# Seven-product channel mixing: the second products of a pair of batches one pass later, a third of them between first products, and raw weights and spills on GpSimd's queue

## The chip, the cores and the metric

The kernel runs on one core of one Trainium2 chip. The core has TensorE (PE; its weight loads are listed apart as PEld), VectorE (DVE), ScalarE (ACT), GpSimd (POOL) and SyncE (SP, here a queue of DMA issues alone). Each takes its instructions in order. The metric is device time in microseconds of one execution, as the median of several; lower is better.

## The reference

Three layers follow one another on float32 data with 4 batches, 448 positions and 768 channels:

```
scores = q @ k^T / 8 - log(448);  x = sigmoid(scores) @ v       # 12 heads of 64
h  = x^T @ U @ V;  u = x + h^T                                  # over positions, rank 32
x2 = u + max(u @ w_ch1, 0) @ w_ch2                              # 768 -> 3072 -> 768
theta = x2 @ w_theta
y  = w_tok_r @ (x2 * cos(theta)) + w_tok_i @ (x2 * sin(theta))
u2 = x2 + y;  out = u2 + max(u2 @ w_ch, 0)
```

The weights arrive as float64. The change concerns the line with w_ch1 and w_ch2, and the conversion of the weights of the layers behind it, which goes on beside it.

## The kernel before

**Precision.** TensorE multiplies fp32r operands. Each float32 operand is split into a high and a low part, and each product is three matmuls: high x high, high x low, low x high (`half_product`, L860 to L868; `Y`, L884 to L902).

**Steps and pairs.** The hidden 3072 channels are handled in 12 steps (i = 0 to 11) of 256. A step needs 256 columns of w_ch1 (two jobs, w1_i_0 and w1_i_1) and 256 rows of w_ch2 (two jobs, w2_i_0 and w2_i_1). The 4 batches are two pairs (pr = 0, 1). One step for one pair is called a pass here; it is the function `phase` (L964). A pass has first products (u @ w_ch1, then relu into tiles h) and second products (h @ w_ch2, added to the resident X): for each of the two batches three pieces `Y(..., e2)` of 12 matmuls, "thirds" here. A third goes into one of two banks y, and VectorE adds it to X (L897).

**Seven products.** Steps 0 and 1 take four plain quadrants a pass. From step 2 on, a pass takes the 2 x 2 block product with seven half products of 9 matmuls (b11, b21, t2, t1, b22, t3, t4) in place of eight. Their left operands b11, t1 and so on are made from w1 by VectorE and ScalarE, with low halves by GpSimd. Their right operands are X's splits, or sums s1 to s4 of X's quarters. The sums are made in steps 0 and 1 and written to DRAM (`s_d`); in each pass `load_s` (L913) reads each of the four sets back, three DMAs of 448 KB a set, into a ring of six tiles, so two sets are in memory at a time. A set's load goes out when the set that held its tiles has been used: s3 after t2 (which uses s1), s2 after t1 (s0), the next pass's s1 after b22, its s0 after t3. The program's names count from zero (s_1_3 is set 3 of pair 1).

**Copies.** Partial sums are kept in PSUM banks a, b and d and are reused. ScalarE copies p1, u2 and p5 out (L997) before the next product goes on accumulating in the same bank; VectorE adds the copy to another bank (`both`, L1001), and `relu` (L870) makes h.

**Conversion jobs.** Every weight is a `Conv` job (L126) with steps. `load` brings the raw words into one of two ws tiles, `size` (ScalarE, L151) makes an estimate of the value, `bits`, `top`, `word` (VectorE, L155 to L165) put the exact float32 together in one of three ca tiles, and a finish makes high and low parts. A job's `load_ahead` issues the raw load of the job two places on; it takes place after `word`, or for theta after the finish, since that job's finish uses the ws tile as scratch. Such a load waits until VectorE has done the step. Extra jobs convert the later layers' weights and spill them to DRAM: 6 for theta, 7 for w_tok, 12 halves of w_ch in 6 jobs. The tables `place` and `place_extra` (L650 to L697) set at which place (i, b, t) of the program a step of a job is recorded, and `tick` records them there.

**Queues.** Behind the attention layer, raw loads, spills, s loads and the writes of s all go out from SP, in program order.

Of the kernel before, what the change touches and what calls it, by code (L numbers as in the profile page):

```python
# [24 lines left out]
def tile_kernel(  # L25
# [101 lines left out]
    class Conv:  # L127
        def __init__(self, key, pp, n, dma, fin, turns=False, more=(), dest=None):
            self.key, self.pp, self.n, self.dma = key, pp, n, dma
            self.turns, self.dest, self.fin = turns, dest, fin  # L130
            self.next = None
            self.steps = [self.size, self.bits, self.top, self.word, *([self.finish] if fin else []), *more]
            self.ahead = self.finish if turns else self.word

        def step(self):
            now = self.steps.pop(0)
            now()
            if now == self.ahead:
                self.load_ahead()
# [66 lines left out]
    def loader():  # L206
        return nc.sync if "sp" in late else nc.gpsimd
# [94 lines left out]
    def conv_wc(kk, s):  # L302
# [55 lines left out]
    def conv_tok(i):  # L358
# [22 lines left out]
        def spill():  # L381
            nc.sync.dma_start(out=tok_d[:, :, i, :], in_=st["o"])
# [264 lines left out]
    extra = th_jobs + [(f"tok{i}", conv_tok(i)) for i in range(NZ)]  # L647
    extra += [(f"wc{kk}_{s}", conv_wc(kk, s)) for kk in range(NH3) for s in range(2)]
# [13 lines left out]
    def place_extra(i, b):  # L662

        name, job = extra.pop(0)
        queue(name, job)
        for t in range(1, 4):
            at(i, b, t, name)
        ts = (0, 2, 4) if job.turns else (0, 2) if len(job.steps) == 6 else (0, 1, 3, 4)
        if not job.turns:
            at(i, b, 4, name)  # L670
        for t in ts:
            at(i, b + 1, t, name)

    place(0, 2, ("w1", 1, 0), conv_w1(1, 0))
    place(0, 3, ("w1", 1, 1), conv_w1(1, 1))
    name = ("w2", 1, 0)
    queue(name, conv_w2(1, 0))
    for t in range(1, 5):
        at(0, 3, t, name)
    at(1, 0, 0, name)  # L680
    for i in range(1, NB):
        more = 1 < i < L
        place(i, 0, ("w2", i, 1), conv_w2(i, 1), (0, 3))
        if more:
            place_extra(i, 0)
        if i == L:
            break
        place(i, 1, ("w2", i + 1, 0), conv_w2(i + 1, 0))
        if more:
            place_extra(i, 1)  # L690
        place(i, 2, ("w1", i + 1, 0), conv_w1(i + 1, 0))
        if i == L - 1:
            place_extra(i, 2)
        name = ("w1", i + 1, 1)
        place(i, 3, name, conv_w1(i + 1, 1))
        if i + 1 >= PLAIN:
            for t in range(2, 5):  # L697
                at(i, 3, t, name)
# [241 lines left out]
    def s_split(n, part):  # L940
        pr, kk = divmod(n, K3)
        (s2, s4), (s3, s1) = ((a[:, 0], a[:, 1]) for a in s_job[n])
        for x, s in (((2, s2), (1, s1)), ((4, s4), (3, s3)))[part]:
# [6 lines left out]
    def do(i, b, t):  # L950
        n = 4 * i + b - 2
        if 0 <= n < 2 * K3:
            if t == 0:
                s_load(n)
            elif t == 2:
                s_sums(n)
            elif t > 2:
                s_split(n, t - 3)
        tick(i, b, t)

    def ticks(i, b):
        return lambda e2: do(i, b, e2 + 2)

    def phase(i, pr, prev):  # L964
        b = 2 * pr

        def last(e2):
            if prev is not None:
                Y(*prev, 1, e2, ticks(i, b))

        def mine(e2):
            Y(i, pr, 0, e2, ticks(i, b + 1))

        if i < PLAIN:
            quadrant(i, pr, 0, 0, lambda: do(i, b, 0))
            quadrant(i, pr, 0, 1, lambda: do(i, b, 1))
            for e2 in range(NK // 2):
                if prev is None:
                    do(i, b, e2 + 2)
                last(e2)  # L980
            quadrant(i, pr, 1, 1, lambda: do(i, b + 1, 0))
            quadrant(i, pr, 1, 0, lambda: do(i, b + 1, 1))
            if i == PLAIN - 1:
                for x in (1, 0)[pr:pr + 1]:
                    load_s(0, x)
            for e2 in range(NK // 2):
                mine(e2)
            return
        w = {x: w1_t[i, x] for x in ("b11", "b21", "b22", "t1", "t2", "t3", "t4")}
# [10 lines left out]
        def both(o, t):  # L1000
            nc.vector.tensor_add(t, o, t)  # L1001
            return t
        a, bb, d = (bank_g(f"{x}_{i}_{pr}") for x in "abd")
# [8 lines left out]
        if (i, pr) == (L, 1):  # L1012
# [5 lines left out]
        if (i, pr) == (L, 1):  # L1018
            load_th(2, False)
        last(1)  # L1020
        half_product(d, w["b22"], xs_q[pr, 3], False)
# [3 lines left out]
        last(2)  # L1025
        half_product(a, w["t3"], xs_q[pr, 2], False)
        if more:
            load_s(nxt[1], 0)
        if (i, pr) == (L, 1):
            load_th(3, False)  # L1030
        relu((i, pr, 1, 1), both(a, p5), lambda: do(i, b + 1, 0))
        mine(0)
        half_product(a, w["t4"], a22, False)
        relu((i, pr, 1, 0), a, lambda: do(i, b + 1, 1))
# [591 lines left out]
```

## Time and profile before

| | us |
|---|---|
| median of 3 runs | 1230.09 |
| lowest, highest | 1225.1, 1232.09 |
| profiled execution | 1226.73 |
| its span | 1223.9 |
| PE busy / PEld busy | 1125.2 / 969.0 |
| DVE busy | 805.1 |
| ACT busy | 444.3 |
| POOL busy | 323.2 |
| TensorE's mean granted clock (1 is full) | 0.970 |

The profile is of one execution. Busy time is the time in which an instruction of the engine ran; matmuls overlap, so PE's busy time says little of how many matmuls ran, and the count beside it says more. PEclk is the granted clock of TensorE in a stretch, as a share of full speed. DMA is the mean busy share of the core's 16 DMA engines. A wait is listed with the engine and line that waited, and with what released it.

### The profile page before, as it was taken

Reading aid. Unit: us, or ns where it says so; the run is one execution under the profiler, and the core shown is the slowest. Engines: PE = TensorE matmul, PEld = TensorE weight load, DVE = VectorE, ACT = ScalarE, POOL = GpSimd, SP = SyncE. Lnnn points to the kernel's source line nnn. Section 1 sums busy time; section 2 is a strip of 40 time slices with the busy share of each in tenths; the row PEclk is TensorE's granted clock in tenths of the full one; section 3 lists DMA queues with packets and bytes.
Section 4 is the critical chain, followed back from the end, with each engine's and each line's share of the span. In section 5 each row is a group of like instructions: output and inputs, shape, how many; then the busy total and the mean of one; then the engine's idle time right before and its main releaser. Section 6 shows DMA issues by size and latency. Waiting matters only on the chain. (4 is left out here: it accounts for less than half of the span.)

```text
span 1223.9 us, 16968 instructions
## 1 busy us (share of the span) xinstructions
PE 1125.2 (92%) x6183; PEld 969.0 (79%) x6183; DVE 805.1 (66%) x1138; ACT 444.3 (36%) x697; POOL 323.2 (26%) x340
## 2 busy tenths in 40 slices
PE   8999989898898989999999989797899999999997
PEld 5554478897777777888888878686798999999997
DVE  5878785877656566656566766567566645564785
ACT  6887752333232222322222233233220534341330
POOL 6412052112121112121212222223312323230273
PEclk9999999899898999999899989899799999999999
DMA  9999527678676778878777786776777732081333
GB/s 169 158 198 189 89 95 248 236 276 342 208 272 204 266 267 273 286 239 285 239 268 256 271 297 246 257 288 226 285 263 276 224 52 40 1 261 36 79 70 71
DMA packets 267794, 254.23 MB, mean 208 GB/s; under 512 B 170928, under 2 KB 222576, under 8 KB 267584
## 3 DMA queue, kind: packets, MB, share of 16 engines
q1 hardware_dynamic: 255600, 231.82, 60.7%
q0 software_dynamic: 8256, 20.87, 6.2%
q10 hardware_dynamic: 3856, 0.48, 0.3%
q8 instruction: 48, 0.79, 0.3%
q14 instruction: 34, 0.28, 0.1%
HBM read 206.83 MB, written 44.89 MB: 206 GB/s over the span
## 5 line engine op out<-in xcount | busy, mean ns | idle before, releaser
L893 PE MATMUL y<-h,w 128*128 128x448 f32 x576 | 215.5, 374 | 15.5 <-DVE X L897 14.9
L894 PE MATMUL y<-h,w 128*128 128x448 f32 x576 | 213.3, 370 | 0.0
L895 PE MATMUL y<-h,w 128*128 128x448 f32 x576 | 213.3, 370 | 0.0
L897 DVE TENSOR_TENSOR X<-y,X 128x896 f32<-128x896 f32 x144 | 156.3, 1086 | 81.8 <-PE y L895 81.5
L893 PEld LDWEIGHTS y<-h,w 128*128 128x128 f32 x576 | 112.4, 195 | 27.5 <-DVE X L897 17.4
L894 PEld LDWEIGHTS y<-h,w 128*128 128x128 f32 x576 | 112.1, 195 | 8.2
L895 PEld LDWEIGHTS y<-h,w 128*128 128x128 f32 x576 | 111.4, 193 | 7.9
L115 POOL TENSOR_TENSOR w<-ca_w,w 128x768 fp32r<-128x768 f32 x22 | 40.8, 1855 | 202.5 <-ACT w L112 202.5
L866 PE MATMUL g_a<-s,w_t 128*128 128x448 f32 x120 | 48.9, 407 | 29.8 <-ACT p L997 23.6
L509 ACT ACTIVATE A<-sc,bias_s 128x896 f32<-128x896 f32 x72 | 70.1, 1013 | 13.9 <-PE sc L527 13.9
L115 POOL TENSOR_TENSOR zl<-t,zh 128x768 fp32r<-128x768 f32 x21 | 40.6, 1952 | 92.6 <-ACT zh L112 67.3
L866 PE MATMUL g_d<-s,w_b 128*128 128x448 f32 x60 | 29.8, 497 | 37.7 <-DMA s<-s_d 37.6
L1275 PE MATMUL y<-tok,zl 128*128 128x448 f32 x168 | 61.0, 363 | 0.0
L1273 PE MATMUL y<-tok,zh 128*128 128x448 f32 x168 | 60.9, 363 | 0.0
L1274 PE MATMUL y<-tok,zh 128*128 128x448 f32 x168 | 60.8, 362 | 0.0
L561 PE MATMUL av<-A,v 128*64 128x448 f32 x288 | 59.4, 548 | 0.7 <-ACT A L509 0.7
L872 ACT ACTIVATE h<-p 128x448 fp32r<-128x448 f32 x40 | 23.2, 580 | 100.2 <-DVE p L1001 100.2
L866 PEld LDWEIGHTS g_d<-s,w_b 128*128 128x128 f32 x60 | 12.4, 207 | 57.1 <-issue 33.5
L159 DVE SCALAR_TENSOR_TENSOR ws_w<-ca_w,ws_w 128x768 uint32<-128x768 uint32 x48 | 55.0, 1146 | 3.4
L866 PEld LDWEIGHTS g_a<-s,w_t 128*128 128x128 f32 x120 | 23.8, 198 | 41.0 <-ACT p L997 27.4
L165 DVE SCALAR_TENSOR_TENSOR ca_w<-ca_w,ws_w 128x768 uint32<-128x768 uint32 x48 | 53.0, 1104 | 3.0
L115 POOL TENSOR_TENSOR w_b<-ca_w,w_b 128x384 fp32r<-128x384 f32 x34 | 35.0, 1045 | 67.8 <-ACT w_b L112 49.6
(293 smaller groups left out, 2742.0 us busy)
## 6 DMA issues: line engine op xcount, KB each, us to landing
s<-s_d SPq DMA_DIRECT2D x240, 448.0 KB, 6.8
ws_w<-in_moe_w_ch_dram SPq DMA_DIRECT2D x42, 768.0 KB, 4.9
x_d<-X SPq DMA_DIRECT2D x4, 1344.0 KB, 5.9
sp_s<-x_d SPq DMA_DIRECT2D x12, 448.0 KB, 4.9
s_d<-s SPq DMA_DIRECT2D x24, 224.0 KB, 2.2
s_d<-sp_s SPq DMA_DIRECT2D x24, 224.0 KB, 2.2
x_d<-stg POOLq DMA_DIRECT2D x24, 224.0 KB, 4.0
q<-in_q_dram SPq DMA_DIRECT2D x90, 56.0 KB, 4.2
```

Of the source, the lines that this page charges most:

```text
L115: nc.gpsimd.tensor_sub(o, a, b)
L159: nc.vector.scalar_tensor_tensor(out=lw, in0=A, scalar=0x80000000, in1=lw, op0=ALU.bitwise_and, op1=ALU.bitwise_or)
L509: nc.scalar.activation(a, ps, AF.Sigmoid, bias=bias_s, scale=SCALE)
L561: nc.tensor.matmul(ps[h * D:(h + 1) * D, :S], v_t[p // 2][:, 2 * (p % 2) + h, c, :], A_t[p, c][:, h, :], start=c == 0, stop=False,)
L866: nc.tensor.matmul(o, wh, xh, start=start and kk == 0, stop=False, skip_group_check=True)
L893: nc.tensor.matmul(ps[:, e], wh, h[:, 0], start=j == 0, stop=False)
L894: nc.tensor.matmul(ps[:, e], wh, h[:, 1], start=False, stop=False)
L895: nc.tensor.matmul(ps[:, e], wl, h[:, 0], start=False, stop=j == FB - 1)
L897: nc.vector.tensor_add(x, ps, x)
L1273: nc.tensor.matmul(o, zh[:, sl], tok_h[:, i, :], start=first and n == 0, stop=False)
L1274: nc.tensor.matmul(o, zh[:, sl], tok_l[:, i, :], start=False, stop=False)
L1275: nc.tensor.matmul(o, zl[:, sl], tok_h[:, i, :], start=False, stop=last and n == len(slots) - 1)
```

## The change

1. `phase` for the seven products: all six thirds of a pass belong to the pair before (both batches), none to the pass's own pair. One third stands after each of b11, t2, b22 and t3, two after t1, and the order of products is b11, t2, b21, t1, b22, t3, t4. `relu` of the first tile stands behind a third. After the last pass all six thirds of its pair follow.
2. The places of conversion steps are counted in 7 steps k a pass (`do(i, pr, k)`). The jobs' places are new; `bits`, `top` and `word` stand at one k. The extra jobs come in the order theta, w_ch, w_tok, and run to step 11.
3. Every job issues the load of the job two places on after `word`. Theta's finish gets a scratch tile of its own from the ring sp for that.
4. Raw loads and spills go out from GpSimd's queue. The s loads, the writes of s and the loads of step 11 stay on SP.
5. In steps 0 and 1 the thirds stand in two blocks of three around the quadrants; the making of the sums is counted in steps of three k. U2 of the last batch uses the banks g, a tile at a time, instead of the banks y.

```diff
-            self.ahead = self.finish if turns else self.word
-            if now == self.ahead:
+            if now == self.word:
                 self.load_ahead()
     def loader():
-        return nc.sync if "sp" in late else nc.gpsimd
+        return nc.gpsimd
-            split_turns(st["h"].bitcast(F32R), a, t)
+            split_turns(st["h"].bitcast(F32R), a, wide(spill_tile(f"{name}_t")))
-                nc.sync.dma_start(out=kept[name][:, n], in_=st[x])
+                nc.gpsimd.dma_start(out=kept[name][:, n], in_=st[x])
...
-    extra = th_jobs + [(f"tok{i}", conv_tok(i)) for i in range(NZ)]
+    extra = th_jobs + extra + toks
...
+    def place(i, pr, name, job, *when):
+        queue(name, job)
+        size, words, *rest = when
+        for k in (size, words, words, words, *rest):
+            ph = 2 * i + pr + k // NT7
+            units.setdefault((ph // 2, ph % 2, k % NT7), []).append(name)
...
+        place(i, 0, ("w2", i, 1), conv_w2(i, 1), 2, 3, 6)
+        place(i, 0, ("w2", i + 1, 0), conv_w2(i + 1, 0), 4, 5, 7)
+        place(i, 1, ("w1", i + 1, 0), conv_w1(i + 1, 0), 0, 1, 2)
...
+        def y(k):
+            Y(*prev, *divmod(k, K3), lambda e2: None)
...
-        half_product(a, w["b11"], xa[0])
+        half_product(a, w1_t[i, "b11"], xa[0])
         p1 = copy(a, "p1")
-        half_product(bb, w["b21"], xa[1])
-        relu((i, pr, 0, 0), both(bb, p1), lambda: do(i, b, 0))
-        half_product(a, w["t2"], xs_q[pr, 1], False)
+        y(0)
+        do(i, pr, 0)
+        half_product(a, w1_t[i, "t2"], xs_q[pr, 1], False)
         load_s(pr, 3)
         u2 = copy(a, "u2")
-        do(i, b, 1)
-        last(0)
-        half_product(d, w["t1"], xs_q[pr, 0])
+        y(1)
+        do(i, pr, 1)
+        half_product(bb, w1_t[i, "b21"], xa[1])
+        c11 = both(bb, p1)
+        half_product(d, w1_t[i, "t1"], xs_q[pr, 0])
         load_s(pr, 2)
         p5 = copy(d, "p5")
-        last(1)
-        half_product(d, w["b22"], xs_q[pr, 3], False)
+        y(2)
+        relu((i, pr, 0, 0), c11)
+        do(i, pr, 2)
+        y(3)
+        do(i, pr, 3)
+        half_product(d, w1_t[i, "b22"], xs_q[pr, 3], False)
...
-    split_x(1)
+    for e2 in range(NK // 2):
+        Y(*prev, 0, e2, lambda e2: e2 == 1 and split_x(1))
```

TensorE, the second pair's pass of step 9, before: the first matmul of each product and third. In g_a_9_1 the last number is the pair; y_9_0_1_0 is step 9, pair 0, batch 1 of the pair, third 0; w1_9_t2 is the operand t2.

```order
L866 MATMUL g_a_9_1_6813<-a_1_0_0_0_2321,w1_9_b11_6376 128x448
...
L866 MATMUL g_b_9_1_6814<-a_1_0_1_0_2348,w1_9_b21_6378 128x448
...
L866 MATMUL g_a_9_1_6813<-s_1_1_0_6678,w1_9_t2_6522 128x448
...
L893 MATMUL y_9_0_1_0_6878<-h_9_0_1_0_6765,w2_9_0_6278 128x448
...
L866 MATMUL g_d_9_1_6815<-s_1_0_0_6717,w1_9_t1_6524 128x448
...
L893 MATMUL y_9_0_1_1_6909<-h_9_0_1_0_6765,w2_9_0_6278 128x448
...
L866 MATMUL g_d_9_1_6815<-s_1_3_0_6862,w1_9_b22_6543 128x448
```

The same place on TensorE in the changed kernel:

```order
L859 MATMUL g_a_9_1_6802<-a_1_0_0_0_2323,w1_9_b11_6438 128x448
...
L886 MATMUL y_9_0_0_0_6816<-h_9_0_0_0_6685,w2_9_0_6350 128x448
...
L859 MATMUL g_a_9_1_6802<-s_1_1_0_6718,w1_9_t2_6541 128x448
...
L886 MATMUL y_9_0_0_1_6852<-h_9_0_0_0_6685,w2_9_0_6350 128x448
...
L859 MATMUL g_b_9_1_6803<-a_1_0_1_0_2352,w1_9_b21_6440 128x448
...
L859 MATMUL g_d_9_1_6804<-s_1_0_0_6753,w1_9_t1_6543 128x448
...
L886 MATMUL y_9_0_0_2_6901<-h_9_0_0_0_6685,w2_9_1_6799 128x448
...
L886 MATMUL y_9_0_1_0_6926<-h_9_0_1_0_6795,w2_9_0_6350 128x448
...
L859 MATMUL g_d_9_1_6804<-s_1_3_0_6844,w1_9_b22_6564 128x448
```

A third stands between b11 and t2, and between t2 (which frees set 1) and b22 (which reads set 3) stand three thirds and two products instead of two thirds and one.

SP's queue at the same place, before. ws_w1_10_1 and ws_w2_10_1 are raw loads, s_1_3 and s_1_2 sets of sums, wc_d1 a spill of w_ch:

```order
L218 DMA ws_w1_10_1_6809<-in_moe_w_ch1_dram 128x6x256
L264 DMA ws_w2_10_1_6850<-in_moe_w_ch2_dram 128x2x768
L917 DMA s_1_3_0_6862<-s_d1_3_2078 128x896
...
L330 DMA wc_d1_73<-sp_wc1_0_b_6839 128x4x192
L330 DMA wc_d1_73<-ca_wc1_0_6754 128x4x192
L917 DMA s_1_2_0_6901<-s_d1_2_2077 128x896
```

SP's queue in the changed kernel, from the set before to set 2 of that pass:

```order
L910 DMA s_1_0_0_6753<-s_d1_0_2075 128x896
...
L910 DMA s_1_3_0_6844<-s_d1_3_2078 128x896
L910 DMA s_1_3_1_6846<-s_d1_3_2078 128x896
L910 DMA s_1_3_2_6848<-s_d1_3_2078 128x896
L910 DMA s_1_2_0_6893<-s_d1_2_2077 128x896
```

Only s loads are left between s loads.

GpSimd's queue around the low half of w2_6_1 (end of step 6's first pass), before:

```order
L115 TENSOR_TENSOR w1_6_b22_5097<-ca_w1_6_1_5017,w1_6_b22_5097 128x384
L115 TENSOR_TENSOR w1_6_t3_5099<-ca_w1_6_1_5017,w1_6_t3_5099 128x384
L115 TENSOR_TENSOR w1_6_t4_5117<-ca_w1_6_0_4877,w1_6_t4_5117 128x384
L115 TENSOR_TENSOR w2_6_1_5219<-ca_w2_6_1_5120,w2_6_1_5219 128x768
L115 TENSOR_TENSOR sp_tok2_5282<-sp_tok2_5282 128x448
```

GpSimd's queue at the same place in the changed kernel:

```order
L217 DMA ws_w1_7_0_5233<-in_moe_w_ch1_dram 128x6x256
L115 TENSOR_TENSOR ca_wc1_0_5127<-ca_wc1_0_5127,sp_wc1_0_b_5303 128x768
L217 DMA ws_w1_7_1_5314<-in_moe_w_ch1_dram 128x6x256
L329 DMA wc_d1_73<-sp_wc1_0_b_5303 128x4x192
L329 DMA wc_d1_73<-ca_wc1_0_5127 128x4x192
L115 TENSOR_TENSOR w2_6_1_5330<-ca_w2_6_1_5212,w2_6_1_5330 128x768
```

The low half of w2_6_1 now stands behind two raw loads and two spills on the same engine.

## Rows read from the trace of the kernel before

**Rows 1.** The page: its head.

```profile
span 1223.9 us, 16968 instructions
```

**Rows 2.** Time by stretch: us, busy us of engines (instructions), PEclk, DMA share, GB/s.

```profile
170.70:278.67 107.97, 99.49 (x475) 90.67 (x476) 80.08 (x105) 33.83 (x62) 28.97 (x23) 0.97 0.67 231
278.67:946.00 667.33, 592.43 (x2734) 525.54 (x2733) 425.79 (x538) 185.66 (x312) 147.06 (x122) 0.95 0.75 264
```

The engines stand in the order PE, PEld, DVE, ACT, POOL.

**Rows 3.** Timeline of TensorE, step 3, second pair: start us, us, engine, instruction, [wait].

```profile
381.98 0.36 PE L867 MATMUL g_b<-a,w_b 128*128 128x448 f32 x1
382.18 0.36 PE L868 MATMUL g_b<-a,w_b 128*128 128x448 f32 x1
388.15 0.74 PE L866 MATMUL g_a<-s,w_t 128*128 128x448 f32 x1 [5.61 <-ACT p L997]
```

**Rows 4.** Time by stretch, three single passes; columns as in rows 2.

```profile
278.67:310.91 32.24, 28.96 (x136) 26.47 (x135) 24.30 (x30) 10.63 (x18) 5.62 (x4) 0.95 0.88 317
...
766.72:805.14 38.42, 29.86 (x136) 26.23 (x135) 23.20 (x30) 11.58 (x20) 10.08 (x8) 0.91 0.83 294
...
882.56:910.13 27.57, 27.57 (x137) 25.79 (x136) 15.26 (x20) 4.83 (x9) 6.89 (x8) 0.98 0.75 262
```

**Rows 5.** Waits of TensorE, 278.6 to 947 us: total us, times, longest us.

```profile
PE g_d L866 <- DMA s<-s_d: 37.6, 44, 6.5
PE g_a L866 <- ACT p L997: 23.6, 10, 5.6
PE y L893 <- DVE X L897: 6.8, 4, 4.8
PE g_a L866 <- DMA s<-s_d: 6.0, 12, 1.7
```

**Rows 6.** Timeline of TensorE, step 9, second pair, before b22.

```profile
787.48 0.71 PE L866 MATMUL g_d<-s,w_b 128*128 128x448 f32 x1 [6.45 <-DMA s<-s_d]
787.99 0.57 PE L867 MATMUL g_d<-s,w_b 128*128 128x448 f32 x1
```

**Rows 7.** Timeline of ScalarE, step 3, second pair.

```profile
383.43 0.92 ACT L151 ACTIVATE ca_th<-ws_th 128x768 f32<-128x768 f32 x1 [11.00 <-DMA ws_th<-in_moe_w_theta_dram]
...
387.58 0.52 ACT L997 COPY p<-g_a 128x448 f32<-128x448 f32 x1
```

**Rows 8.** Timeline of SP's queue, step 9, second pair.

```profile
773.47 0.46 SPq L218 DMA_DIRECT2D ws_w<-in_moe_w_ch_dram  x1
781.52 0.37 SPq L264 DMA_DIRECT2D ws_w<-in_moe_w_ch_dram  x1
781.99 1.67 SPq L917 DMA_DIRECT2D s<-s_d  x3
```

**Rows 9.** DMA issues of the whole span: count, KB each, median us to landing.

```profile
s<-s_d SPq DMA_DIRECT2D x240, 448.0 KB, 6.8
...
x_d<-stg POOLq DMA_DIRECT2D x24, 224.0 KB, 4.0
...
ws_w<-in_moe_w_ch_dram POOLq DMA_DIRECT2D x6, 768.0 KB, 5.8
```

**Rows 10.** DMA in all, 278 to 947 us.

```profile
DMA packets 90712, 176.79 MB, mean 264 GB/s; under 512 B 18879, under 2 KB 52415, under 8 KB 90675
```

**Rows 11.** Instruction groups, 278.6 to 947 us (last: whole span): busy us, mean ns, idle.

```profile
L897 DVE TENSOR_TENSOR X<-y,X 128x896 f32<-128x896 f32 x125 | 135.6, 1086 | 72.3 <-PE y L895 72.0
L159 DVE SCALAR_TENSOR_TENSOR ws_w<-ca_w,ws_w 128x768 uint32<-128x768 uint32 x37 | 44.5, 1202 | 2.5
L875 DVE SCALAR_TENSOR_TENSOR h<-p,h 128x448 fp32r<-128x448 f32 x40 | 24.7, 618 | 2.0 <-ACT h L872 2.0
...
L115 POOL TENSOR_TENSOR w<-ca_w,w 128x768 fp32r<-128x768 f32 x19 | 34.8, 1829 | 174.8 <-ACT w L112 174.8
...
L264 POOL DMA_DIRECT2D ws_w<-in_moe_w_ch_dram x2 | 1.4, 722 | 5.5 <-ACT A L509 5.5
```

**Rows 12.** Waits of SP's queue: total us, times, longest us.

```profile
SPq L264 <- DVE ca_w L165: 165.4, 17, 14.2
```

More of the change, by code (lines that the diff above doesn't have):

```diff
@@ L660, in place @@
         at(i, b + last[0], last[1], name)
-    def place_extra(i, b):
-        name, job = extra.pop(0)
[L665 to L680, printed above, removed]
+    NT7 = 7
+    def place(i, pr, name, job, *when):
[4 more added lines that the diff above has]
+            units.setdefault((ph // 2, ph % 2, k % NT7), []).append(name)
+        assert len(job.steps) == 4 + len(rest)
+    def place_extra(i, pr, k0, k1, k2):
+        name, job = extra.pop(0)
+        more = (k2,) if len(job.steps) == 5 else (k2, k2 + 1) if len(job.steps) == 6 else (k2, k2 + 1, k2 + 3, k2 + 4)
+        place(i, pr, name, job, k0, k1, *more)
@@ L689, in tile_kernel @@
[L689 to L698, printed above, removed]
+        place(i, 0, ("w2", i + 1, 0), conv_w2(i + 1, 0), 4, 5, 7)
+        place(i, 1, ("w1", i + 1, 0), conv_w1(i + 1, 0), 0, 1, 2)
+        ends = (6,) if i + 1 < PLAIN else (4, 6, 6, 7) if i + 1 == PLAIN else (4, 5, 6, 7)
@@ L699, in tile_kernel @@
+        place(i, 1, ("w1", i + 1, 1), conv_w1(i + 1, 1), 2, 3, *ends)
+        if i > 1:
+            place_extra(i, 1, 4, 5, 6)
     assert not extra
@@ L948, in s_split, with do @@
             nc.sync.dma_start(out=s_d[pr, x - 1][:, kk, 1], in_=s)
[L950 to L953, printed above, removed]
-                s_load(n)
[L955 to L962, printed above, removed]
-    def phase(i, pr, prev):
[L965 to L972, printed above, removed]
-        if i < PLAIN:
[L975 to L982, printed above, removed]
+    def do(i, pr, k):
+        g = NT7 * (2 * i + pr - 1) + k - 2
+        if i < PLAIN and g >= 0:
+            n, r = divmod(g, 3)
+            if r == 2 and n < 2 * K3:
+                s_sums(n)
+            elif r == 0 and n:
+                s_split(n - 1)
+            if r == 0 and n < 2 * K3:
+                s_load(n)
+        tick(i, pr, k)
+    def phase(i, pr, prev):
+        def y(k):
+            Y(*prev, *divmod(k, K3), lambda e2: None)
+        if i < PLAIN:
+            for k in range(2 * K3):
+                if k == K3:
+                    quadrant(i, pr, 0, 0)
+                    quadrant(i, pr, 0, 1)
+                y(k)
+                do(i, pr, k)
+            quadrant(i, pr, 1, 1)
+            quadrant(i, pr, 1, 0)
+            do(i, pr, 6)
             if i == PLAIN - 1:
[L984 to L987, printed above, removed]
+                load_s(0, (1, 0)[pr])
             return
-        w = {x: w1_t[i, x] for x in ("b11", "b21", "b22", "t1", "t2", "t3", "t4")}
         xa = {kh: xa_t[pr, t, kh] for t, kh in ((0, 0), (0, 1))}
@@ L1082, in early_1 @@
     def early_1(e2):
-        ps = ps_y.tile([P, 2, 512], F32, tag="y", name=f"hl_{e2}", bufs=2)
-        U2(B - 1, 2 * e2, ps, vml)
+        for m in range(2):
+            U2(B - 1, 2 * e2 + m, ps_g.tile([P, 1, 512], F32, tag="g", name=f"hl_{e2}_{m}", bufs=4), vml, 1)
         for d in (2 * e2, 2 * e2 + 1):
             split_a(l1, "a", 9, 1, 0, d // K3, (d % K3,), lo_pool)
-        do(0, 1, e2 + 2)
     for e2 in range(NK // 2):
```

63 lines of the change are left out of this document (36 added, 27 removed).

## The prediction

> **What bounds the kernel now.** I read the page first, then the time by stage, then who waits for whom in the longest stage, then single waits on three queues. The profiled execution took 1226.73 us with a span of 1223.9 us [rows 1], so 2.8 us lie around the span; the median shown is 1230.09 us, 3.4 us more. I do the sum on the profiled execution and add the 3.4 us at the end.
>
> The change touches the time from 170.7 us on. The stretch to 278.7 us (steps 0 and 1) takes 108 us; the stretch from 278.7 to 946 us (steps 2 to 11, twenty passes of the seven-product scheme) takes 667.3 us, more than half of the span [rows 2]. By the code a pass is 7 x 9 + 6 x 12 = 135 matmuls, and 36 follow the last pass: 2736 in all, and the row counts 2734. Where TensorE runs undisturbed, matmuls start 0.20 us apart (381.98, then 382.18) [rows 3]. 2736 x 0.20 = 547.2 us, so **120.1 us of this stage are not work of TensorE**. A pass that the trace shows nearly without a gap took 27.57 us, against 135 x 0.20 = 27.0; one with trouble took 38.42 [rows 4].
>
> The waits of TensorE in the stage name 74.0 us of the 120: 37.6 + 6.0 us for loads of the sums s (the seven-product operands that lie in DRAM), 23.6 us for ScalarE's copy p, 6.8 us for VectorE's addition to X [rows 5]. The other 46 us are what follows a wait. The mean granted clock is 0.95 [rows 2], so a tenth of the stage, 67 us, ran at 1.2 GHz instead of 2.4; a matmul then takes 0.57 us in the record, right after a wait, instead of 0.36 [rows 3, 6]. And the pipeline refills after each of the 60 waits. I count these 46 us to the waits before them.
>
> The two large waits have causes that can be seen. The copy p: TensorE stood 5.61 us before t2 [rows 3], since ScalarE, which works in order, had waited 11.00 us for the raw theta weights; it then did three other things and began its copy at 387.58 [rows 7]. The s load: TensorE stood 6.45 us for s3 before b22 [rows 6], but the three loads had gone out only at 781.99. SP's queue stood from 773.93 to 781.52 in front of a raw weight load, which waits for VectorE's last conversion step [rows 8]. TensorE could run 5.5 us after the issue: the transfer was not slow, its issue was late.
>
> **The change, part by part.**
>
> *Product order (all passes).* No matmul is added. The copy p1 now has a third of a second product over it, 12 x 0.20 = 2.4 us, where b21 gave 9 x 0.20 = 1.8. The window of s3 (end of t2 to b22) grows from third, t1, third = 33 matmuls = 6.6 us to third, b21, t1, third, third = 54 = 10.8 us; that of s2 (end of t1 to t3) from 6.6 to third, third, b22, third = 45 = 9.0 us. The median landing of an s load is 6.8 us from issue [rows 9]: formerly 0.2 us too long, now with 4.0 and 2.2 us to spare. The windows of s1 and s0 shrink (16.8 to 12.6, 16.8 to 14.4 us) and stay far above it. An addition to X takes 1.09 us [rows 11] and now has 4.2 us or more (a third and a product) until its bank is wanted; I take its 6.8 us as gone.
>
> *The p copies.* A theta load was issued at the end of the job two before; now it goes out with the word step, for all jobs alike. From there to the step in which ScalarE reads it are 3 or 4 of a pass's 7 steps, 3/7 x 27 = 11.6 us or more, against a landing of 5.8 us for raw loads on GpSimd's queue [rows 9]. I take all 23.6 us as gone. If that cover failed, ScalarE would again stand before its copies, though TensorE now wants u2 and p5 only 20 or more matmuls later.
>
> *GpSimd's queue.* It holds 105 instructions more, nearly all of them DMA issues; at 0.72 us [rows 11] that is 76 us in a stage in which GpSimd is busy for 147 us of 667 [rows 2]. SP loses as many, and nothing that waits for VectorE stands before its s loads any more.
> The Trainium skill's page "DMA: Bandwidth & Descriptors", section "Issuing engines are not separate DMA queues", says that DMAs issued from several engines share the same DMA engines, and that a second issuing engine saves only the sequencer's time. What SP lost was time of its sequencer, 7.6 us at one place [rows 8], so read in this way the rule leaves the sum as it is; read strictly (no better service of the s loads), it is the second rival below.
>
> *What a wait on GpSimd holds up.* Behind a raw load that waits for VectorE stand the low halves that GpSimd subtracts. The tight one is that of w2_i_1, used in the middle of the second third of the pair's second pass. From step 5 on VectorE does X, 1.09, a low part of h, 0.62, a finish of two steps and three conversion steps, each at most 1.20; then GpSimd issues the load and two spills, 3 x 0.72, and subtracts, 1.83 [rows 11]. Together 11.7 us. TensorE has t4, b11, a third, t2 and half a third until then: 45 x 0.20 = 9.0 us. That is short by 2.7 us at worst, and by nothing when the finish is short: bounds 0 and 27 us over ten such passes; I take **15 us**, since these means include stretched instructions.
>
> *Bandwidth.* The stage moved 176.79 MB [rows 10]. In 547 us that would be 323 GB/s; the highest rate that a whole pass held is 317 GB/s, at a DMA share of 0.88. At 317 it takes 558 us; at 294, the pass at 766.72 with its spills of w_ch, 601 us [rows 4]. Bounds 0 and 54 us; I take **10 us**, nearest to 317, since the rate of the other pass was held down by a queue that stood.
>
> *The end.* Three more y pieces stand behind the last pass, with six transposes through three buffers; their stores land 4.0 us after issue [rows 9], so a buffer turns in about 5 us and the six need 10 us, beside 36 + 36 matmuls (14.4 us). **2 us**, bounds 0 and 6.
>
> *Steps 0 and 1.* The same matmuls, 36 of them moved into the next stage, and U2 on other banks; VectorE is busy 80 of 108 us there [rows 2]. I take no change, bounds -5 and +5.
>
> **Sum:** 120.1 - 15 - 10 - 2 = 93 us. 1226.7 - 93 = 1133.7; with the 3.4 us, **1137 us**. Its own range, from none of the 27 us to twice as much: 1110 to 1164.
>
> **Rivals.**
> 1. *Transfers become the pace.* The stage falls only to what 294 GB/s allow, 601 us, and the shortfall on GpSimd lies within these waits: 667.3 - 601 = 66 us less, 2 us for the end, 1230 - 66 + 2 = 1166. For it: the demand of 323 lies above every pass seen. Against: 317 went at a share of 0.88, not 1. Chance 0.18.
> 2. *The s loads are no better served.* Raw loads of 768 KB run beside the s loads instead of behind them and take half of the rate away: the 43.6 us of s waits stay with their share of the rest, 43.6 x 120/74 = 71 us. Gain 120 - 71 - 15 = 34 us; 1196. Against: the longer windows. Chance 0.07.
> 3. *GpSimd's in-order queue becomes the bound, and the kernel is slower.* Place: the three raw loads of each pass, each of which waits for VectorE's word step. SP spent 165.4 us in 17 such waits, up to 14.2 us each [rows 12]; now GpSimd spends them, with spills and low halves behind. The low halves of w1 and w2 and the next raw loads come late, ScalarE waits for those loads, and its copies p are late again. It decides from 93/20 = 4.7 us lost per pass; at 7.5 us, half of such a longest wait, 1137 + 150 = 1287. Against: the waits on SP began early because SP had nothing else to do, and only one deadline is short by the sum above. Chance 0.10.
> The Trainium skill's page "SBUF — State Buffer", section "SBUF: two separate sides", speaks for this rival: while VectorE holds the port pair that it shares with GpSimd, GpSimd cannot write descriptors, and a DMA from its queue starts late. The trace shows six raw loads from that queue landing after 5.8 us, an s load from SP after 6.8 [rows 9]: so far no sign of it.
>
> **Chances.** Forecast 0.65, rivals 0.18, 0.07, 0.10. Half a per cent, 6 us, is about what can be told from no change. Only the third rival ends above 1224, a little of it within 6 us of 1230: slower 0.08, within 0.5% 0.03 with the tail of the second, faster 0.89. The range 1110 to 1196 takes in the first rival and half of the second, and leaves out about 0.17.
>
> **What would show it.** Right: passes of 27 to 29 us, a granted clock of 0.98 or more in the stage, waits for s below 15 us and nearly none for p, SP waiting only for TensorE before s loads, the stage at 300 GB/s or more. The 15 us would show as y waiting for w from GpSimd in second passes. Wrong: TensorE waiting for s at a DMA share above 0.9 (first rival) or below it (second); GpSimd idle before raw loads on VectorE's word step, with ScalarE waiting for those loads (third).

## The result, and the profile after

The changed kernel took **1167.91 us** (median of 4 runs, 1165.7 to 1169.09), the kernel before beside it 1227.59 us; the ratio is 0.951, with a 95% interval of 0.947 to 0.9551. The forecast was 1137 us: the direction and the range held, the size did not. The profiled execution took 1169.09 us with a span of 1167.2, 56.7 us less than the span before [rows 1].

First the time by stretch of the kernel after (columns as in rows 2), cut at the start of step 2 (287.68; the first row ends 0.3 us behind it) and at the start of the layer behind:

```profile
170.00:288.00 118.00, 98.38 (x458) 88.77 (x459) 81.41 (x108) 35.48 (x66) 31.89 (x29) 0.91 0.60 210
287.68:889.90 602.22, 567.44 (x2765) 521.61 (x2764) 444.21 (x542) 183.79 (x315) 237.70 (x248) 0.99 0.85 293
889.90:1167.20 277.30, 269.86 (x1510) 262.40 (x1508) 171.01 (x269) 98.27 (x149) 90.90 (x103) 0.99 0.38 96
```

Step 2 now begins with 2772 matmuls left in the stage (2736 and the 36 that the change moves there). The kernel before had that many left 36 x 0.20 = 7.2 us before its step 2, at 271.5 us. So the same three stretches of the kernel before are:

```profile
170.70:271.50 100.80, 92.92 (x443) 84.86 (x444) 74.59 (x96) 32.89 (x60) 26.83 (x21) 0.97 0.66 227
271.50:946.80 675.30, 599.77 (x2769) 531.73 (x2767) 431.28 (x547) 186.60 (x314) 149.20 (x124) 0.95 0.75 264
946.80:1223.90 277.10, 268.24 (x1500) 260.84 (x1500) 168.16 (x268) 98.26 (x149) 91.94 (x103) 1.00 0.37 93
```

Three differences add up here: the stage (steps 2 to 11) is 73.1 us shorter, step 2 begins 16.2 us later (287.68 against 271.5), the end is the same: 73.1 - 16.2 - 0.2 = 56.7 us. Not all of the 16.2 us lies in steps 0 and 1. Their first third begins at 170.68 us before and at 174.40 after, and the code up to there is the same in both kernels; in the twelve other profiles of this record that third begins between 170.9 and 176.9 us. So 3.7 us are a difference between two executions ahead of the changed part, and steps 0 and 1 themselves are 12.5 us longer. In the stage 2772 x 0.20 = 554.4 us are work; of 120.9 us beside it 47.8 are left. The clock is at 0.99 of full speed, where it was 0.95.

Then who waits, for TensorE in steps 0 to 11 after (total us, times, longest us). Rows 5 begin only with step 2; in this list the waits for X and h and 1.4 us of those for w lie in steps 0 and 1:

```profile
PE g_a L859 <- ACT p L980: 12.3, 10, 7.4
PE g_a L859 <- DVE p L984: 12.2, 10, 1.7
PE y L888 <- POOL w L115: 11.6, 9, 2.5
PE y L886 <- DVE X L890: 11.4, 3, 9.1
PE y L886 <- ACT h L865: 3.9, 2, 3.3
PE y L887 <- DVE h L868: 2.5, 1, 2.5
```

Not one wait for an s load is left, where there were 43.6 us [rows 5]. SP now stands before s loads for TensorE's use of the tiles (`SPq L910 <- PE g_a L861: 242.8, 114, 11.2` the largest) and no longer for VectorE [rows 8, 12]. Three single passes, first pair, second pair and first pair, answer to rows 4:

```profile
589.10:616.90 27.80, 27.22 (x136) 25.21 (x135) 23.50 (x27) 9.71 (x16) 13.59 (x14) 1.00 0.91 327
616.90:649.80 32.90, 29.21 (x137) 26.55 (x137) 23.46 (x32) 10.36 (x17) 18.15 (x18) 0.95 0.91 304
763.50:791.30 27.80, 27.28 (x136) 25.25 (x136) 17.40 (x24) 7.68 (x14) 8.60 (x10) 1.00 0.85 279
```

A pass now moves its data at 327 GB/s, above any pass before, and still takes 27.8 us. First passes take 27.8 to 27.9 us, apart from step 2's 36.9. Second passes take 29 us, and 32.6 to 32.9 in steps 5 to 7, where w_ch is spilled.

### The profile page after: what moved, and what is told of

It reads as the page before. It is cut to its first block, busy times and chain, and to the rows that moved or that the text cites. A ratio compares the mean times of both kernels' runs of the same rounds, so it can differ in the third digit from the quotient of the medians.

```text
span 1167.2 us, 17018 instructions
## 1 busy us (share of the span) xinstructions
PE 1098.2 (94%) x6183; PEld 962.2 (82%) x6183; DVE 824.3 (71%) x1141; ACT 440.7 (38%) x697; POOL 415.1 (36%) x471
## 5 line engine op out<-in xcount | busy, mean ns | idle before, releaser
L886 PE MATMUL y<-h,w 128*128 128x448 f32 x576 | 211.5, 367 | 15.2 <-DVE X L890 11.4
L888 PE MATMUL y<-h,w 128*128 128x448 f32 x576 | 212.4, 369 | 11.6 <-POOL w L115 11.6
L887 PE MATMUL y<-h,w 128*128 128x448 f32 x576 | 210.7, 366 | 2.5 <-DVE h L868 2.5
L886 PEld LDWEIGHTS y<-h,w 128*128 128x128 f32 x576 | 109.7, 190 | 24.0 <-DVE X L890 12.5
L888 PEld LDWEIGHTS y<-h,w 128*128 128x128 f32 x576 | 109.6, 190 | 22.4 <-POOL w L115 15.2
L887 PEld LDWEIGHTS y<-h,w 128*128 128x128 f32 x576 | 109.6, 190 | 10.8 <-DVE h L868 2.9
L217 POOL DMA_DIRECT2D ws_w<-in_moe_w_ch_dram x24 | 20.3, 847 | 142.0 <-issue 36.9
L859 PE MATMUL g_a<-s,w_t 128*128 128x448 f32 x120 | 45.4, 378 | 12.3 <-ACT p L980 12.3
L865 ACT ACTIVATE h<-u 128x448 fp32r<-128x448 f32 x20 | 11.6, 578 | 114.5 <-DVE u L984 114.5
L150 ACT ACTIVATE ca_w<-ws_w 128x768 f32<-128x768 f32 x48 | 43.1, 897 | 27.8 <-POOL w L115 22.2
L158 DVE SCALAR_TENSOR_TENSOR ws_w<-ca_w,ws_w 128x768 uint32<-128x768 uint32 x48 | 50.7, 1055 | 4.0
L164 DVE SCALAR_TENSOR_TENSOR ca_w<-ca_w,ws_w 128x768 uint32<-128x768 uint32 x48 | 49.0, 1021 | 3.8
L1278 DVE TENSOR_TENSOR X<-y,X 128x448 f32<-128x448 f32 (+2 forms) x36 | 15.6, 464 | 48.9 <-PE y L1272 48.8
L1438 POOL DMA_DIRECT2D out_dram<-o x45 | 27.5, 618 | 63.5 <-DVE o L1449 58.8
```

The source lines that it names most:

```text
L158: nc.vector.scalar_tensor_tensor(out=lw, in0=A, scalar=0x80000000, in1=lw, op0=ALU.bitwise_and, op1=ALU.bitwise_or)
L164: nc.vector.scalar_tensor_tensor(out=A if self.dest is None else self.dest(), in0=A, scalar=3, in1=lw, op0=ALU.logical_shift_left, op1=ALU ...
L859: nc.tensor.matmul(o, wh, xh, start=start and kk == 0, stop=False, skip_group_check=True)
L886: nc.tensor.matmul(ps[:, e], wh, h[:, 0], start=j == 0, stop=False)
L887: nc.tensor.matmul(ps[:, e], wh, h[:, 1], start=False, stop=False)
L888: nc.tensor.matmul(ps[:, e], wl, h[:, 0], start=False, stop=j == FB - 1)
```

## Three places where time is lost after

**Steps 0 and 1.** VectorE and TensorE (start us, us, engine, instruction, [wait]):

```profile
256.54 0.63 DVE L928 TENSOR_TENSOR sp_s<-sp_s 128x448 f32<-128x448 f32 x1 [8.74 <-DMA sp_s<-x_d]
...
259.06 1.08 DVE L890 TENSOR_TENSOR X<-y,X 128x896 f32<-128x896 f32 x1
```
```profile
250.72 0.37 PE L888 MATMUL y<-h,w 128*128 128x448 f32 x1
260.20 0.74 PE L886 MATMUL y<-h,w 128*128 128x448 f32 x1 [9.11 <-DVE X L890]
```

VectorE works in order and stands 8.74 us at the first sum of a quarter, whose load has not landed. Behind it stands the addition to X that would free TensorE's bank. The quarters share two tiles, so each goes round one chain: split, write to DRAM, next load, landing (5.6 us in the median), sums. Rounds start 15 to 21 us apart (loads issued at 197.34, 212.73, 229.07 and 249.65 us); the change gives them three counts, of which some lie in a block of thirds, 2.4 us apart. The last quarter's round runs on into step 2: ScalarE makes its four high halves from 291.95 us on, and the copy p that the first t2 waits for begins only behind them, at 298.92. TensorE stands 7.43 us there.

**Middle of a second pass.** GpSimd, then TensorE, in step 7:

```profile
622.75 0.85 POOL L217 DMA_DIRECT2D ws_w<-in_moe_w_ch_dram  x1 [2.43 <-DVE h L868]
623.60 0.77 POOL L329 DMA_DIRECT2D wc_d<-sp_wc_b  x1
624.36 0.76 POOL L329 DMA_DIRECT2D wc_d<-ca_wc  x1
625.13 3.61 POOL L115 TENSOR_TENSOR w<-ca_w,w 128x768 fp32r<-128x768 f32 x2
```
```profile
627.00 0.47 PE L888 MATMUL y<-h,w 128*128 128x448 f32 x1 [2.31 <-POOL w L115]
...
628.58 0.57 PE L859 MATMUL g_b<-a,w_b 128*128 128x448 f32 x1
```

This is the low half of w2_i_1 behind a raw load and two spills, as the prediction described it. The wait is 2.31 us; from 628.3 to 631.9 us ten matmuls then start 0.36 us apart in the mean instead of 0.20, at a granted clock of 0.53 (1.2 GHz for nearly all of them), which is 1.6 us more. Steps 5, 6 and 7 have such waits (2.50, 2.00, 2.31 us); five other second passes have 0.2 to 1.0 us.

**End of a second pass.** VectorE in step 7, and TensorE:

```profile
645.17 0.55 DVE L245 TENSOR_TENSOR ca_w<-ca_w,ca_w 128x384 f32<-128x384 f32 x1
...
646.70 0.55 DVE L248 TENSOR_TENSOR ca_w<-ca_w,t 128x384 f32<-128x384 f32 x1
647.17 0.62 DVE L984 TENSOR_TENSOR p<-g_a,p 128x448 f32<-128x448 f32 x1
```
```profile
647.84 0.47 PE L859 MATMUL g_a<-a,w_t 128*128 128x448 f32 x1 [1.37 <-DVE p L984]
```

The four sums for the next step's w1 stand ahead of the addition that makes c22, and t4 may begin only behind it.

## The experiments

**One: the queues.** The changed kernel with raw loads and spills on SP again:

```diff
     def loader():
-        return nc.gpsimd
+        return nc.sync if "sp" in late else nc.gpsimd
...
-                nc.gpsimd.dma_start(     # the spills of theta, w_ch, w_tok
+                nc.sync.dma_start(
```

> The changed kernel with raw loads and spills back on SP's queue: the new product order and conversion places alone. Theory (the order with its longer windows does most of the work, SP's standing the rest): the waits for the copy p stay small, a part of the waits for s comes back, 5 to 25 us of them with what follows, so 1173 to 1193 us against 1168. Rival (taking loads off SP's queue did most): the s waits of 44 us come back in full, and with the clock some 70 us, 1215 us or more.

Measured: **1153.7 us**, ratio 0.9385 [0.9359, 0.9411], 14 us less than the change. Waits of TensorE:

```profile
PE g_a L859 <- ACT p L980: 19.5, 10, 7.1
PE y L886 <- DVE X L890: 8.8, 4, 5.9
PE g_a L859 <- DVE p L984: 5.7, 7, 2.0
PE g_a L859 <- DMA s<-s_d: 1.6, 7, 0.3
PE y L888 <- POOL w L115: 1.3, 1, 1.3
```

I had expected 1173 to 1193 us and 5 to 25 us of s waits. SP stands before raw loads for VectorE as it did (`SPq L217 <- DVE ca_w`: 131.3 us in 20 waits), and yet the s loads come in time, so the queue isn't needed for that. In the kernel before, the first load of set 3 went out 3.1 us after t2 had freed its tile (median of the twenty passes; 9.3 at worst); here it goes out 1.9 us late (3.8 at worst), and lands 1.2 us or more ahead of b22, in a window that is 4.2 us longer by the prediction's count (10.8 us against 6.6). So the longer windows carry most passes, and the new places of the conversions take away the worst delays; no run has the one without the other. Waits for GpSimd's low halves fall from 11.6 to 1.3 us. By stretch, steps 2 to 11 are 9.2 us shorter than in the changed kernel, steps 0 and 1 5.4 us.

**Two: the queue without the order.** The kernel before with that edit the other way round.

> The kernel before with raw loads and spills on GpSimd's queue and nothing else changed: the queue alone. Theory: SP no longer stands before s loads, but the windows of 6.6 us are as short as the landing and theta's raw load is still issued after its finish, so half of the s waits and most of the p waits stay: 1195 to 1220 us. Rival (the queue did most): s waits below 10 us, 1175 us or less. Third possibility: GpSimd's in-order waits cost more than SP's, slower than 1228.

Measured: 1214.37 us, ratio 0.9879 [0.9851, 0.9908]. Waits of TensorE, 278 to 950 us:

```profile
PE g_a L866 <- ACT p L997: 23.5, 7, 5.8
PE g_d L866 <- ACT p L997: 16.0, 2, 8.3
PE y L893 <- DVE X L897: 15.3, 8, 6.9
PE g_a L866 <- DMA s<-s_d: 8.8, 10, 1.8
```

In the old order the queue takes the s waits from 43.6 to 9.4 us (0.6 us stand in a line not shown), and gives back 16 us of it as waits for p [rows 5]. The time lies in the range that I gave the theory, 1195 to 1220 us, but by luck: the theory had half of the s waits stay and no new waits for p. Step 2 begins at 291.7 us here, against 278.7 before. By stretch, steps 2 to 11 are 27 us shorter than before and steps 0 and 1 10.6 us longer (4.8 us of the waits for X above are theirs). So the same edit gains 15 us in all in the old order, where an s load stood behind a raw load, and costs 14 in the new; to steps 0 and 1 it adds time in both orders.

**Three: theta's load alone**, in the kernel before:

```diff
-            self.ahead = self.finish if turns else self.word
-            if now == self.ahead:
+            if now == self.word:
-            split_turns(st["h"].bitcast(F32R), a, t)
+            split_turns(st["h"].bitcast(F32R), a, wide(spill_tile(f"{name}_t")))
```

> The kernel before with one part of the change alone: theta's next raw load at the word step and with a scratch tile of its own, all on SP's queue, old order of products. Theory (the late raw load of theta and the one third between products are separate; in the old order the waits are for s transfers): within 5 us of the kernel before, 1225 to 1233 us, waits for s at 40 us or more. Rival (theta's late load is what made p1 and X late in the old order): 1212 to 1220 us.

Measured: 1209.31 us, ratio 0.9834 [0.9804, 0.9864]. My theory was wrong by 16 us and the rival nearer, 3 us short of the time:

```profile
PE g_d L865 <- DMA s<-s_d: 40.6, 45, 6.6
PE y L892 <- DVE X L896: 15.1, 10, 5.0
PE g_a L865 <- ACT p L996: 9.6, 7, 3.3
```

The s waits stay, the waits for p fall from 23.6 to 9.6 us, and those for X stay too (14.9 us before in this window, which takes in steps 0 and 1). 14 us of named waits are worth 18 us. If the shares multiply, which no run shows, the ratio of the first experiment leaves 0.9385 / 0.9834 = 0.954, some 56 us, for the rest of that kernel: the order of products, the places for conversions and the new layout of steps 0 and 1.

**Four: when the quarters are loaded.** Sums and split together, the next load at once, three counts to land:

```diff
+            if g == 0:
+                s_load(0)
             if r == 2 and n < 2 * K3:
                 s_sums(n)
-            elif r == 0 and n:
-                s_split(n - 1)
-            if r == 0 and n < 2 * K3:
-                s_load(n)
+                s_split(n)
+                if n + 1 < 2 * K3:
+                    s_load(n + 1)
```

> The changed kernel, but in steps 0 and 1 the sums are split right after they are made and the load of the next quarters goes out then, three counts before they are used instead of two. Theory (steps 0 and 1 lost time because VectorE stood, in order, before sums whose quarters had not landed, and additions to X stood behind): the longest wait of y for X (9.1 us) and the 7.4 us before the first t2 shrink, 10 to 25 us less, 1143 to 1158 us. Rival (VectorE has too much to do in the thirds of these steps, and does not wait): no change, 1165 to 1171.

Measured: 1168.88 us, ratio 0.9501 [0.948, 0.9521], no change. The wait went to ScalarE, whose high halves of the sums stand in its order ahead of what TensorE needs:

```profile
PE g L859 <- ACT a L112: 10.5, 1, 10.5
PE y L886 <- ACT w L112: 9.0, 1, 9.0
```

A second form spread the quarters over counts 0 to 22, into step 2:

```diff
+    S_LOAD, S_SUM, S_SPLIT = (0, 4, 7, 11, 15, 19), (3, 7, 10, 14, 18, 21), (4, 7, 11, 15, 19, 22)
...
```

> The changed kernel with another spread of the six s quarters of steps 0 and 1: the last one is loaded at count 19 of the stage and split at count 22 (in the first pass of step 2) where the changed kernel ends at count 18, so that most loads have three counts to land, the second quarter's with thirds and all four quadrants between. Theory (a quarter's chain of write, load, sums and split takes about 16 us against three counts of about 4 us, and VectorE stands in written order at the sums): waits of TensorE for X, h and p between 190 and 300 us fall from about 24 us to under 10, and the time to 1150 to 1158 us. Rival (steps 0 and 1 are paced by transfers or by GpSimd's queue, not by these waits): 1164 to 1170 us, with the waits named otherwise.

Measured: 1163.93 us, ratio 0.9462 [0.9429, 0.9496]: 4 us, not 10 to 18. Waits for X fell from 11.4 to 2.8 us, and one wait of 9.0 us for c22 came up in step 2, since the split there shares a ring of three tiles with the copies p1, u2 and p5: ScalarE stood 7.48 us, by the profile for a write of s. Steps 0 and 1 were 10.0 us shorter than in the changed kernel, and the first pass of step 2 took 45.3 us instead of 36.9. So the early loss is a chain that goes round two tiles and passes three in-order engines; moving its steps moved the wait. No run has more tiles or a shorter chain.

**Five: GpSimd's low half one count earlier.**

```diff
-        place(i, 0, ("w2", i, 1), conv_w2(i, 1), 2, 3, 6)
+        place(i, 0, ("w2", i, 1), conv_w2(i, 1), 2, 3, 5)
```

> The changed kernel with the finish of w2_i_1 at k = 5 instead of 6, so that its low half stands before the raw load that waits for VectorE. Theory (the 10.2 us in which y waits for w from GpSimd in second passes come from that place in the queue): these waits vanish, and with refills and clock 10 to 17 us less, 1151 to 1158 us. Rival (GpSimd is late as a whole, by its DMA issues): the wait shrinks by less than 4 us, 1163 to 1168 us.

Measured: 1161.5 us, ratio 0.9443 [0.9416, 0.9471]. The waits for GpSimd are gone from the list; those for c22 rose (`PE g_a L859 <- DVE p L984: 15.9, 8, 3.7`), since TensorE now gets there sooner. 6.4 us were won, where 10 to 17 were expected.

**Six: the w1 sums behind c22.**

```diff
         y(4)
-        do(i, pr, 4)
...
         c22 = both(a, p5)
+        do(i, pr, 4)
         y(5)
```

> The changed kernel with one move: in each pass of steps 2 to 11 the conversion step at count 4 (in second passes the four w1 sums on VectorE, 0.55 us each) is recorded behind the addition that makes c22, no longer ahead of it. Theory (VectorE's written order makes the fourth seven-product operand late): the waits of TensorE for g_d<-DVE p, 12.2 us in ten second passes, go; 1168 - 12 = 1156 us, 1153 to 1160. Rival (the sums, now later, make the t operands later by as much, and the waits move to the conversion): 1166 to 1170 us. Second rival (second passes are paced by GpSimd's low halves, 11.6 us in nine passes, which the c22 wait only covers): the wait for w2_i_1 grows and 4 us or less are won.

Measured: 1160.65 us, ratio 0.9434 [0.9405, 0.9464]: 7 us of the 12. In the profiled executions steps 2 to 11, where the edit is, are only 4.1 us shorter; another 3.5 us lie ahead of steps 0 and 1, in code that the edit leaves as it was. The c22 waits fell from 12.2 to 1.8, and those for p1 rose to 18.4: VectorE's later steps now make a conversion late whose high half ScalarE takes just ahead of p1.

**Seven: together.** SP's queue, the c22 edit and the wide spread; the second kernel has the earlier low half too.

> Raw loads and spills on SP's queue again (1153.7 us alone), the count-4 step behind c22, and the other spread of the s quarters, all three. Theory (three separate losses that add up): 1153.7 less 5 (its c22 waits were 5.7 us) less 10 to 16 = 1133 to 1139 us. Rival (with the early waits gone the stage is paced by transfers at about 300 GB/s, and waits for s come back): 1143 to 1152 us with waits for s over 10 us.

> The kernel with all three edits and, beside them, the low half of w2_i_1 recorded one count earlier. Theory: with SP's queue only 1.3 us of waits for GpSimd's low halves were left, so nothing is to be had here: within 2 us of the kernel with three edits. Rival (the sums' move hands the wait to GpSimd, whose low halves then come late): 4 to 8 us faster than it.

Measured: 1163.76 us, ratio 0.9471 [0.9444, 0.9499], and 1163.57 [0.9438, 0.9485]. The sum failed: both are slower than the first experiment alone. No transfer rate explains it: the pass at 613.70 below ran at 325 GB/s in 27.9 us. In the first of these kernels two things cost more than the edits won. The first pass of step 2 took 45.3 us (35.7 in the first experiment), with a wait of 9.7 us for c22 as in the spread alone. And the nine first passes behind it took 16 us more in all, since their waits for p1 rose from 1.2 to 1.4 us in most to 2.0 to 2.3. Two of them, each with one wait for p1 (TensorE; then by stretch, with the second pass between them):

```profile
589.16 0.47 PE L859 MATMUL g_a<-s,w_t 128*128 128x448 f32 x1 [2.19 <-ACT p L980]
```
```profile
648.06 0.47 PE L859 MATMUL g_a<-s,w_t 128*128 128x448 f32 x1 [2.08 <-ACT p L980]
```
```profile
582.60:613.70 31.10, 28.91 (x137) 26.61 (x137) 22.66 (x28) 9.74 (x16) 9.01 (x6) 0.95 0.90 307
613.70:641.60 27.90, 27.52 (x136) 25.11 (x135) 24.52 (x30) 10.05 (x17) 11.74 (x8) 1.00 0.94 325
641.60:671.00 29.40, 27.32 (x137) 25.25 (x137) 21.69 (x28) 8.69 (x15) 8.91 (x6) 1.00 0.95 323
```

0.1 us more of a wait, 1.7 us more of a pass: behind the longer one ten matmuls ran at 1.2 GHz (0.58 us in the record), behind the shorter none. The length of the wait alone doesn't decide it. In the kernel of experiment six, a pass with one wait of 1.86 us took 30.7 us at a granted clock of 0.94, and a pass with one wait of 2.50 us took 30.0 at full clock (by stretch):

```profile
519.12:549.84 30.72, 28.86 (x136) 26.55 (x135) 24.71 (x30) 9.92 (x17) 13.75 (x14) 0.94 0.88 305
489.10:519.12 30.02, 27.52 (x137) 25.15 (x135) 22.41 (x30) 10.28 (x17) 17.51 (x16) 1.00 0.87 310
```

In the first experiment the p1 waits were 1.2 to 1.4 us in most passes and cost some 0.3 us beside themselves.

**Eight: what stands ahead of p1.** ScalarE in that kernel:

```profile
761.67 0.58 ACT L112 ACTIVATE sp_tok<-sp_tok 128x448 fp32r<-128x448 f32 x1 [3.93 <-DVE sp_tok L376]
762.15 0.52 ACT L980 COPY p<-g_a 128x448 f32<-128x448 f32 x1
```

The high half of an extra conversion, which waits for VectorE, stands right ahead of the copy. So SP's queue, the c22 edit, and that finish one count later; the second kernel has beside it a tighter spread within steps 0 and 1:

```diff
-            place_extra(i, 1, 4, 5, 6)
+            place_extra(i, 1, 4, 5, 7)
```

> Raw loads and spills on SP's queue again (1153.7 us alone), the count-4 step behind c22, and the extra conversion of a second pass finished one count later, so that ScalarE's high half of it no longer stands ahead of the copy of p1. Theory (the copy of p1 waits in ScalarE's written order behind that high half, which waits for VectorE; waits of 2.2 us are moreover followed by some ten matmuls at 0.36 us): the waits of TensorE for p1 in the first passes from step 3 on (1.2 us each with SP's queue, 2.2 with the c22 edit beside it) go, both kinds of passes take 27.0 to 27.4 us, and the time is 1153.7 less 5 less 12 to 15 = 1134 to 1138 us. Rival (the copy is late because TensorE's previous product frees late, not by ScalarE's order): p1 waits stay at 1 us or more, 1148 to 1166 us.

> The same kernel, and beside it the six s quarters of steps 0 and 1 loaded at counts 0, 3, 4, 8, 12, 15 of the stage and summed and split together at 3, 4, 8, 12, 15, 18, so that quadrants (7 to 14 us of TensorE) lie in five of the six gaps and nothing reaches step 2. Theory (early waits come from the landing of these loads, which the blocks of thirds are too short for): waits for X, h and p between 190 and 300 us fall by 8 to 14 us, and the time by as much against the kernel without it. Rival (the waits only move to ScalarE, as with sums at an even three counts): within 3 us of it.

Measured: 1156.89 us, ratio 0.9426 [0.94, 0.9453], and 1156.99 [0.9408, 0.9443]. The time lies in the range of the rival, but not for its reason: fifteen of the first nineteen passes took 27.0 to 28.1 us, as the theory had it. Three, the second passes of steps 6 to 8, each behind the split of a w_ch conversion, took 35.1 to 37.2, which I had not foreseen (ScalarE):

```profile
543.39 0.84 ACT L112 ACTIVATE sp_wc_b<-ca_wc 128x768 fp32r<-128x768 f32 x1 [9.04 <-DMA wc_d<-sp_wc_h]
...
545.29 0.52 ACT L980 COPY p<-g_a 128x448 f32<-128x448 f32 x1
```

ScalarE stands 9.04 us at a tile whose spill has not landed: SP issued it at 533.47 us, and ScalarE wanted the tile from 534.35 on. By the later finish the spill goes out just before the tile is wanted again. The spread of the second kernel gained nothing.

**Nine: the same, but for w_ch.**

```diff
-            place_extra(i, 1, 4, 5, 7)
+            place_extra(i, 1, 4, 5, 6 if extra[0][0].startswith("wc") else 7)
```

> The kernel with SP's queue, the c22 edit and the later finish of the extra conversion in second passes, but for the three w_ch conversions of second passes, which finish where they did. Theory (with the later finish sixteen of twenty passes took 27.0 to 28.1 us; three, behind a w_ch conversion moved into the pass that splits the next, took 35 to 37 us because ScalarE stood at the spill of the conversion before, 9.0 us, with the copy of p1 behind it): those three return to 27 us, and the three first passes after a w_ch conversion wait up to 2.2 us for p1 again, with the slow matmuls behind it, up to 4 us each. 1157 less 27 plus 4 to 12 = 1134 to 1142 us. Rival (the 35 us passes come from the raw data of w_ch, whatever the place of its finish): 1152 to 1160 us.

Measured: **1138.33 us** (1135.34 to 1141.99), ratio 0.9261 [0.922, 0.9303], the fastest of all kernels here, 30 us below the change and within the 1134 to 1142 us expected. Waits of TensorE, and three of its passes by stretch:

```profile
PE g_a L859 <- ACT p L980: 13.9, 4, 7.4
PE y L886 <- DVE X L890: 8.9, 4, 5.8
PE g_a L859 <- DVE p L984: 2.1, 1, 2.1
```
```profile
683.60:710.60 27.00, 27.00 (x136) 25.31 (x135) 19.81 (x26) 7.68 (x14) 5.54 (x5) 1.00 0.85 319
710.60:737.60 27.00, 27.00 (x136) 25.31 (x135) 20.56 (x28) 9.56 (x17) 9.56 (x7) 1.00 0.85 276
568.20:599.40 31.20, 28.82 (x136) 26.50 (x135) 22.75 (x28) 9.74 (x16) 7.82 (x6) 0.95 0.91 305
```

Most passes are now all work, 135 x 0.20 = 27.0 us. Left in this stage are above all the first pass of step 2 (37.4 us) and three passes behind a w_ch conversion (29.4, 31.2 and 29.4 us).

## Why the prediction was right in direction and 31 us short

- **s loads: right.** 43.6 us expected gone, all gone; the first experiment shows that the queue wasn't needed for it, and experiment three that theta's early load alone doesn't do it. Between the longer windows and the new places of the conversions no run separates. (Rows 5 hold 70 waits, not the 60 of the prediction; nothing hangs on it.)
- **p copies: right for theta.** 23.6 us expected gone. After, 12.3 us stand there by the same name, from two other causes: 7.4 in the first pass of step 2 (the last quarter's high halves on ScalarE, above), and 0.5 us in each of nine first passes. The share of theta alone is 14 us of waits and 18 us of time (experiment three).
- **GpSimd, 15 us: right in place, and 10.2 us in size.** The worst was 2.50 us against the 2.7 worked out, and it came where the spills are. What I didn't price are the matmuls at 1.2 GHz that followed these waits: second passes of steps 5 to 7 took 32.6 to 32.9 us after, and 28.3 to 28.8 with SP's queue.
- **Bandwidth, 10 us: nothing.** TensorE waits for no DMA after, at up to 327 GB/s in a pass. (The stage as a whole moved 293 GB/s, short of the 300 named as a sign, since it was longer than forecast.) The first rival, with its 1166 us, came near the time for a reason that did not occur.
- **The end, 2 us: nothing** (277.3 against 277.1).
- **Steps 0 and 1, "no change, bounds -5 and +5": the step that failed.** They took 12.5 us more (the other 3.7 of the 16.2 us lie ahead of them), and left the first pass of step 2 at 36.9 us, 9 above its like. I counted the busy time of VectorE and the matmuls, and did not ask where VectorE stands in order when a load has not landed. Two parts of the change bear on it. With the quarters spread over other counts steps 0 and 1 were 10.0 us shorter, though step 2 gave 8 of it back (experiment four). With SP's queue again they were 5.4 us shorter (experiment one), and in the old order GpSimd's queue alone made them 10.6 us longer (experiment two). With both edits the gain was 10.1 us (12.9 in the second kernel of experiment seven), so the two don't add up. How the queue does it is open: the quarters' loads landed after 5.6 us in the median with raw loads on GpSimd and 4.1 with SP, and in the old order after 5.8 and 4.9.
- **Not in the sum at all: c22.** Four sums of 0.55 us ahead of it cost 12.2 us of waits in ten passes.

So the forecast's 93 us less 56.7 leaves 36.3 by the spans: 12.5 in steps 0 and 1 and 3.7 ahead of them; in the stage 47.8 us left instead of 25, of 120.9 instead of 120.1, which is 22.0; less 1.8 at the end. The miss of 31 us by the medians is smaller since the profiled execution after lies 1.2 us above its median, where the forecast put the median 3.4 above the profiled execution, and 0.9 us less lies around the span. The second rival (s loads no better served) did not occur. The third (GpSimd's queue as the bound) did in small: it costs 14 us, not 150. By the profiled executions 5.4 us lie in steps 0 and 1 and 9.2 in the stage, where second passes, with the one tight deadline, take 19 us more in all and first passes 8 less.

The Trainium skill's page "DMA: Bandwidth & Descriptors", section "Issuing engines are not separate DMA queues", says that DMAs started by different engines run on the same DMA engines, and that starting them from several saves only the sequencer's time to initiate them. The trace agrees as far as the transfers go: in the old order an s load landed 6.2 us after its issue (median) with the raw loads on GpSimd and 6.8 with them on SP [rows 9]. What the queue won there was not time to initiate a DMA but time that SP stood in order, 7.6 us ahead of one s load [rows 8]; in the new order hardly any TensorE wait hung on that (1.6 us in experiment one), and GpSimd's own work paid.

## What to carry to other kernels

After moving work, list for each in-order engine what stands directly ahead of the instruction that the bounding engine waits for, and for what that in turn waits: the losses here (sums ahead of X, w1 sums ahead of c22, an extra's high half ahead of p1, a spill ahead of w2's low half, a tile's spill ahead of p1) are one pattern, and three small edits (SP's queue, the w1 sums, the extra's finish) won 30 us. Try the parts of a change alone: one of its three parts cost 14 us where the others stood. A fix of one wait here often only uncovered the next on another engine, so the waits that the edits removed didn't add up. And compare stretches that begin at the same instruction: the code ahead of the change differed by up to 6 us between the executions here.

## What the runs showed that I had not expected

- A wait's price is not smooth, and its length alone doesn't set it. First passes with one wait of 2.08 us took 29.4 us in two kernels and 30.9 in a third (the second of experiment seven), there with matmuls at 1.2 GHz behind it. In the changed kernel and in experiments one and six, no pass whose longest wait was 1.7 us or less had such matmuls; in experiment six one with 1.86 had them, and one with 2.50 had not.
- A raw load of w_ch1 or w_ch2 (768 KB) took 7.3 us from issue to landing on GpSimd's queue after (48 of them, median) and 5.2 on SP's in the first experiment (42). In the old order it took 6.4 on GpSimd's (48) and 4.9 on SP's (42). What makes the difference was not separated.
